# Retention attention into a SoLU layer: a negated copy of h with a row maximum, variance by squares on ScalarE, new engine orders

## The chip, the core and the metric

The kernel runs on one core of a Trainium2 chip. The metric is the device time of one execution in microseconds, the median of the runs shown. A core has a matrix engine (PE, with its weight load PEld), VectorE (DVE), ScalarE (ACT), GpSimd (POOL) and a sync engine (SP) that here only issues transfers. Each engine executes its own queue in order; instructions of different engines wait for one another by semaphores. [...]

## What is computed

Inputs `q`, `k`, `v` are 8 batches x 8 heads x 576 positions x 64, all float32. The reference, cut to what matters:

```python
scores = scale * np.matmul(q, k.transpose(0, 1, 3, 2))
ret = scores * Dmat            # causal, gamma_h ** (i - j)
x = (ret @ v), heads side by side            # 4608 x 512
h = x @ w_in                                 # 4608 x 1024
e = np.exp(h - h_max)                        # h_max: row maximum
solu = h * (e / (np.sum(e) + 1e-09))
ln = (solu - mu) / np.sqrt(var + 1e-06) * g_ln
out = ln @ w_out                             # 4608 x 512
```

The layer norm cancels any common factor of a row, so the kernel never divides by the sum of the exponentials: it carries `h * e` and scales the `1e-6` by the square of that sum.

## The kernel before, in words

The 4608 rows are cut into 18 windows: for each batch two windows of 256 positions, and for each four batches one window that collects their last 64 positions. A window has two **streams** (the two halves of the heads, 36 in all, number i) and two **token tiles** (128 rows each, 36 in all, number t).

The steps of a stream are named by letters in the code. `ldq`, `ldk`, `ldv` load 256 KB each (SP). `sq`, `sk` scale q and k by powers of gamma to f16, `cv` casts v; they run on POOL (for the first two streams `sq` is on DVE and `cv` on ACT). `T` transposes q and k (PE), `qe` copies them out (ACT), `S` makes scores (PE), `mask` multiplies them by the causal mask (DVE, line 382), `K` makes the state of a window (PE), `sa`, `sd` add it up (DVE), `sm`, `sc` scale and cast it (POOL), `I` and `V` make the output (PE), `xe` copies it out as `xT` (ACT).

The steps of a token tile:

- `M1` (PE, line 434): eight 128x512 products fill the PSUM tile `h`, of which there is one buffer.
- `ex` (ACT, line 447): `e = exp(h)` read from PSUM, with the row sum `se`.
- `so` (DVE, line 454): `solu = h * e` in f16, one input in PSUM and one in SBUF. It ends the use of `h`: the next tile's `M1` waits for it.
- `bn` (DVE, lines 460 and 464): two `bn_stats` and one `bn_aggr` give the mean and the variance. After the second tile of a window, two small instructions of 128x2 (lines 468 and 471) put variance and `1e-6 * se * se` together.
- `rs` (POOL, line 477): the power -1/2.
- `L` (PE, line 483) transposes `solu`, `le` (ACT) copies it out, `M2` (PE, line 507) multiplies by the output weights.
- `od` (DVE, line 515), for the first `NE` = 14 tiles only: takes the mean times the column sums of the weights (`nws`) off the product. From tile 14 on the weights themselves are centred (`w2c16`), and `od` falls away. `oe` (ACT, line 523) scales by `rs`, `out` (SP) stores.

The output weights are made ready beside the first tiles: `wg` multiplies the rows by the gain (four on DVE, four on ACT), `WM` sums the columns on PE, `nw0`, `nw1` copy the sums out (ACT), `wf` scales the float32 weights again (ACT, eight times) and `wp` adds the sums (POOL, line 578, eight times).

What stands in which order on an engine is decided when the program is built. Every step is an `op(name, engine, kind, deps, key, emit, bufs)`; an engine's steps are sorted by key and go into its queue in that order. The key is a formula in periods, or, for the steps listed in `FIRST`, their place in a list written out by hand. `order_ops` only merges the queues. Before, the lists cover roughly tiles 0 to 14, and the rest goes by formula. A buffer count (`CAP`) and the steps that release a buffer make further waits.

Of the kernel before, what the change touches and what calls it, by code (L numbers as in the profile page):

```python
# [9 lines left out]
FP = mybir.dt.float32  # L10
F16 = mybir.dt.float16
P = 128
# [4 lines left out]
    qe=0.6, xe=0.59, ex=1.22, le=0.6, oe=0.69, wi=0.6, wg=0.66, cva=0.6,  # L17
    mask=1.22, st_a=0.29, so=1.22, bn=1.68, od=0.7, wib=0.55, wgd=0.5, WM=1.73, nw=0.62, wf=0.66, wp=1.04, sqd=0.7, gc=0.2,
    sq=1.03, sk=1.03, st_b=0.4, cast=0.84, rs=0.6, cv=0.61,
# [6 lines left out]
NE = 14  # L26

FIRST = dict(
    ACT=(
        "cv0 qe0 cv1 qe1 xe0 wi1a wi2a wi0a xe1 wi3a ex0 qe2 wg0 le0 wg2 qe3 wg4 wg6 ex1 xe2 "  # L30
        "nw1 nw0 xe3 qe4 wf1 ex2 qe5 wf3 le1 xe4 qe6 wf2 ex3 le2 xe5 oe0 qe7 wf0 ex4 le3 xe6 "
        "qe8 ex5 le4 xe7 qe9 oe1 ex6 le5 oe2 qe10 xe8 ex7 le6 xe9 qe11 oe3 ex8 le7 oe4 wf6 "
        "qe12 xe10 wf4 ex9 le8 xe11 oe5 wf7 qe13 ex10 le9 xe12 wf5 qe14 oe6 ex11 le10 xe13 "
        "oe7 qe15 oe8 ex12 le11 xe14 qe16 oe9 ex13 le12 xe15 qe17 oe10 ex14 le13"
    ),
    DVE=(
        "gc sq0 sa0 sd0 sq1 mask0 wi1b sa1 sd1 mask1 wi2b wi0b wi3b sa2 sd2 so0 mask2 wg1 sa3 "
        "sd3 wg3 wg5 wg7 mask3 so1 bn0 sa4 sd4 bn1 mask4 so2 od0 sa5 sd5 mask5 bn2 sa6 sd6 "
        "so3 mask6 od1 bn3 sa7 sd7 so4 mask7 od2 bn4 sa8 sd8 so5 mask8 bn5 sa9 sd9 so6 od3 "
        "mask9 bn6 so7 od4 sa10 sd10 mask10 bn7 so8 od5 sa11 sd11 mask11 bn8 sa12 so9 sd12 "  # L40
        "od6 mask12 bn9 sa13 sd13 so10 od7 mask13 bn10 so11 sa14 sd14 od8 bn11 mask14 so12 "
        "sa15 sd15 od9 mask15 bn12 so13 od10 mask16 bn13 so14"
    ),
    PE=(
        "G K0 T0 S0 T1 I0 V0 K1 S1 I1 V1 M1_0 T2 K2 S2 L0 I2 V2 K3 T3 M1_1 S3 WM I3 V3 K4 T4 "
        "M1_2 S4 T5 M2_0 L1 I4 V4 K5 S5 T6 M1_3 I5 V5 K6 S6 L2 M2_1 T7 M1_4 I6 V6 K7 S7 L3 "
        "M2_2 T8 M1_5 I7 V7 K8 S8 L4 M2_3 T9 M1_6 I8 V8 K9 L5 S9 T10 M1_7 L6 I9 M2_4 V9 K10 "
        "S10 T11 M1_8 L7 I10 M2_5 V10 K11 S11 T12 M1_9 L8 I11 V11 K12 S12 M2_6 T13 M1_10 I12 "
        "V12 K13 S13 L9 M2_7 T14 M1_11 I13 L10 M2_8 V13 K14 S14 T15 M1_12 L11 M2_9 I14 V14 "
        "K15 S15 T16 M1_13 L12 I15 S16 V15 M2_10 T17 M1_14 L13 I16 S17 V16 M2_11"  # L50
    ),
    POOL=(
        "sk0 sk1 sm0 sc0 sm1 sc1 sq2 sk2 cv2 sk3 sm2 sc2 cv3 sq3 sm3 sc3 sk4 sq4 cv4 sq5 sk5 "
        "sm4 sc4 sq6 rs0 cv5 sk6 sq7 sm5 sc5 cv6 cv7 sk7 sm6 sk9 sc6 sk8 sq8 wp0 rs1 sm7 sc7 "
        "cv8 sq9 cv10 cv9 wp3 sm8 sk10 sc8 cv12 wp2 sq10 sq11 sq12 sm9 sc9 sk11 cv11 sk12 wp1 "
        "sm10 sc10 sk13 rs2 sq13 sq14 cv14 sm11 sc11 sk14 rs3 wp6 sm12 sc12 cv13 sq16 cv15 "
        "cv16 sm13 sc13 wp4 sk15 sq15 sk16 wp5 rs4 sm14 sc14 sq17 wp7 sk17 rs5 cv17 sm15 sc15 "
        "sq18 sk18 cv18 sq19 sk19 cv19"
    ),
    SP=(  # L60
        "ldk0 ldv0 ldq0 ldk1 ldq1 lm ldv1 lwi1 lwi2 lwi0 lwi3 ldq2 ldk2 ldv2 ldk3 lwo0 ldv3 "
        "ldq3 lwo2 lwo4 lwo6 ldk4 ldq4 ldv4 ldq5 ldk5 ldq6 ldv5 ldk6 ldv7 ldq7 ldq9 ldk7 ldk8 "
        "ldv6 ldq10 ldv8 ldk9 ldq11 ldq8 ldv10 ldk10 ldv11 ldq14 ldk11 ldk14 ldv9 ldv12 ldq12 "
        "ldk12 ldk13 ldq16 out0 out1 ldk17 ldv16 ldq15 ldq13 ldv13 out2 ldv14 ldq17 ldk16 "
        "out4 ldv15 ldk15 out3 out5 out7 out6 ldv17 ldv18 ldq19 ldk18 ldv19 ldq18 ldk19 ldq20 "
        "out8 ldk20 ldv20 out9 ldq21 ldk21 ldv21"
# [107 lines left out]
def kernel(  # L174
# [21 lines left out]
               xT=5, h=1, e=2, oc=2, solu=3, sml=8, lnT=4, o=1, osb=3)  # L196
# [28 lines left out]
    nws = const.tile([P, 2, DM], FP)  # L225
# [213 lines left out]

    def exp_(t):  # L440
        d = tk[t]
        w, c = divmod(t, 2)
        d["e"] = pools["e"].tile([P, DFF], FP, tag="e", name="e_sb")
        if c == 0:
            ws[w]["se"] = pools["sml"].tile([P, 2], FP, tag="se", name="se")
            ws[w]["mv"] = pools["sml"].tile([P, 2, 2], FP, tag="mv", name="mv")
        nc.scalar.activation(  # L447
            out=d["e"], in_=d["h"], func=ACT.Exp, accum_out=ws[w]["se"][:, c : c + 1]
        )

    def solu(t):
        d = tk[t]
        d["solu"] = pools["solu"].tile([P, DFF], F16, tag="solu", name="solu")
        nc.vector.tensor_tensor(out=d["solu"], in0=d["h"], in1=d["e"], op=ALU.mult)  # L454

    def stats(t):
        w, c = divmod(t, 2)
        bs = pools["sml"].tile([P, 2, 6], FP, tag="bs", name="bs")
        for half in range(2):
            nc.vector.bn_stats(  # L460
                out=bs[:, half], in_=tk[t]["solu"][:, half * 512 : half * 512 + 512]
            )
        d = ws[w]
        nc.vector.bn_aggr(out=d["mv"][:, c], in_=bs)
        if c:
            x = pools["sml"].tile([P, 2], FP, tag="w", name="w")
            d["x2"] = pools["sml"].tile([P, 2], FP, tag="w2", name="w2")
            nc.vector.scalar_tensor_tensor(  # L468
                out=x, in0=d["se"], scalar=1e-6, in1=d["se"], op0=ALU.mult, op1=ALU.mult
            )  # L470
            nc.vector.tensor_tensor(out=d["x2"], in0=x, in1=d["mv"][:, :, 1], op=ALU.add)  # L471
# [39 lines left out]
    def o_mean(t):  # L511

        d = tk[t]
        d["oc"] = pools["oc"].tile([P, DM], FP, tag="oc", name="oc")
        nc.vector.scalar_tensor_tensor(  # L515
            out=d["oc"], in0=nws[:, 0], scalar=ws[t // 2]["mv"][:, t % 2, 0:1], in1=d["o"],
            op0=ALU.mult, op1=ALU.add,
        )
# [58 lines left out]
    def w2_center(x):  # L577
        nc.gpsimd.tensor_tensor(out=w2c16[:, x], in0=w2_f[:, x], in1=nws[:, 1], op=ALU.add)
# [46 lines left out]
    for t in range(NT):  # L625
        w, c = divmod(t, 2)
        m = t + 2
        op(f"M1_{t}", "PE", "M1", [f"xe{2 * w}", f"xe{2 * w + 1}"] + [f"wi{x}{y}" for x in range(4) for y in "ab"],
           (m, 3.18), lambda t=t: mm1(t), [("h", [f"so{t}"])])
        op(f"ex{t}", "ACT", "ex", [f"M1_{t}"], (m, 5.1), lambda t=t: exp_(t), [("e", [f"so{t}"])])  # L630
        op(f"so{t}", "DVE", "so", [f"ex{t}"], (m + 1, 1.03), lambda t=t: solu(t), [("solu", [f"L{t}", f"bn{t}"])])
        op(f"bn{t}", "DVE", "bn", [f"so{t}", f"bn{t - 1}" if c else ""], (m + 1, 4.5), lambda t=t: stats(t))
        if c:
            op(f"rs{w}", "POOL", "rs", [f"bn{t - 1}", f"bn{t}"], (m + 2, 0.77), lambda w=w: rstd(w), [("sml", [f"oe{t}"])])
        op(f"L{t}", "PE", "L", [f"so{t}"], (m + 1, 4.9), lambda t=t: ln_tp(t), [("tp", [f"le{t}"])])
        op(f"le{t}", "ACT", "le", [f"L{t}"], (m + 2, 0.97), lambda t=t: ln_ev(t), [("lnT", [f"M2_{t}"])])
        o_end = f"od{t}" if t < NE else f"oe{t}"
        op(f"M2_{t}", "PE", "M2", [f"le{t}"] + [f"{'wg' if t < NE else 'wp'}{x}" for x in range(8)], (m + 4, 1.0),
           lambda t=t: mm2(t), [("s" if late(t) else "o", [o_end])])
        if t < NE:  # L640
            op(o_end, "DVE", "od", [f"M2_{t}", "nw0"], (m + 4, 2.9), lambda t=t: o_mean(t), [("oc", [f"oe{t}"])])
        op(f"oe{t}", "ACT", "oe", [o_end if t < NE else f"M2_{t}", f"rs{w}"], (m + 4, 3.6 if t < NE else 2.9),
           lambda t=t: o_ev(t), [("osb", [f"out{t}"])])
        op(f"out{t}", "SP", "out", [f"oe{t}"], (m + 4, 4.4 if t < NE else 3.6), lambda t=t: store(t))
# [8 lines left out]
    op("gc", "DVE", "gc", ["G"], (0, 1.0), lambda: nc.vector.tensor_copy(out=gln, in_=cur["g_ps"][:, 0:8]))  # L653
    for c in range(0, 8, 2):
        op(f"lwo{c}", "SP", "ldw", [], (-2 + c / 8, 0.6), lambda c=c: nc.sync.dma_start(out=w2_f[:, c : c + 2], in_=w2_v[:, c : c + 2]))
        for x in (c, c + 1):
            op(f"wf{x}", "ACT", "wf", ["gc", "nw1"], (8 + x * 0.75, 1.9), lambda x=x: nc.scalar.activation(
                out=w2_f[:, x], in_=w2_f[:, x], func=ACT.Copy, scale=gln[:, x : x + 1]))
            op(f"wp{x}", "POOL", "wp", [f"wf{x}"], (9 + x * 0.75, 1.9), lambda x=x: w2_center(x))
# [14 lines left out]
    with tc.manual_schedule():  # L674
# [4 lines left out]
        nc.vector.memset(minus1, -1.0)  # L679
# [3 lines left out]
        nc.vector.memset(warm, 0.0)  # L683
# [43 lines left out]
```

## Time and profile before

| | |
|---|---|
| runs | 227.62, 225.35, 226.4 us; median 226.4 |
| span of the profiled execution, first to last instruction | 225.6 us |
| mean granted PE clock | 0.988 |
| DMA | 42.64 MB, 189 GB/s over the span |
| `M1` of tile 0 / 3 / 15 / 31 / 35 starts at | 15.28 / 37.04 / 106.60 / 191.65 / 210.65 us |
| `ex` (line 447), 128x1024 from PSUM | 1022 ns, and 194 ns for reading out its row sum |
| `mask` (line 382), 128x1024 | 1215 ns |
| `od` (line 515), 128x512 | 740 ns |
| `wp` on POOL (line 578), 128x512 | 1268 ns |
| `sq`, `sk` on POOL (line 274) / `cv` (line 282) | 1040 / 608 ns |
| `sm` (line 407) / each half of `sc` (line 416) / `rs` (line 477) on POOL | 418 / 400 / 691 ns |

Beyond its span the page has no time for the profiled execution itself; the span lies 0.8 us under the median of the runs. The busy shares are averages over a start, a stretch in which tiles come irregularly, a regular stretch and an end, so the start times of `M1` are used to cut the span into stages. An instruction's duration counts from when its engine took it up, so it includes time in which it was held; back to back, DVE and ACT instructions start about 0.09 us before the end of the one ahead.

### The profile page before, as it was taken

How to read it: one execution, taken by the hardware profiler on the slowest of the kernel's cores; microseconds unless marked ns; L12 is line 12 of the kernel's file. 1: busy time of each engine (PE TensorE's matmuls, PEld its weight loads, DVE VectorE, ACT ScalarE, POOL GpSimd, SP SyncE). 2: the span in 40 equal slices, each digit the busy share in tenths (PEclk: the TensorE clock that was granted, in tenths of full speed). 3: DMA queues.
4: the chain of work that ended last, by engine and by line, in shares of the span. 5: the costliest groups of instructions: out<-in, count | busy, mean ns of one | idle time of the engine just before them, and what ended most of it. 6: DMA issues, size and time to landing. Idle time of an engine off the chain costs nothing.

```text
span 225.6 us, 7375 instructions
## 1 busy us (share of the span) xinstructions
PE 208.6 (92%) x2983; PEld 122.0 (54%) x2983; DVE 180.0 (80%) x320; ACT 133.2 (59%) x238; POOL 151.6 (67%) x231
## 2 busy tenths in 40 slices
PE   7876989999699999699999999999999999999991
PEld 2423555656355655465665666666566666555440
DVE  6655798999969898999999877778888888876540
ACT  2454776656457876466666566666665556655641
POOL 3439599999959989929669869695968777311010
PEclk9999999999799999999999999999999999999998
DMA  6999999995594600799987777777764552222334
GB/s 178 351 346 346 326 289 289 293 293 135 132 264 109 191 11 3 179 300 310 294 225 202 236 195 205 202 193 193 209 190 107 145 141 53 49 47 60 84 71 117
DMA packets 65635, 42.64 MB, mean 189 GB/s; under 512 B 4024, under 2 KB 59456, under 8 KB 65600
## 3 DMA queue, kind: packets, MB, share of 16 engines
q1 hardware_dynamic: 65200, 41.96, 67.7%
q8 instruction: 23, 0.38, 0.8%
q10 hardware_dynamic: 400, 0.21, 0.6%
q14 instruction: 12, 0.10, 0.2%
HBM read 32.71 MB, written 9.44 MB: 187 GB/s over the span
## 4 chain that ended last, share of the span: by engine, by line
PE 65%; DVE 17%; DMA 5%; POOL 4%; SPq 4%; issue 2%; ACT 1%; DVEq 0%; POOLq 0%; ACTq 0%
PE h_ps L434 22%; PE o_ps L507 21%; PE xy L314 7%; PE tln L483 5%; PE tqk L291 5%; DVE solu L454 4%; PE s_ps L349 4%; DVE bs L460 3%; DVE ret L382 3%; DMA vr<-in_v_dram 3%; SPq L259 3%; DMA masks<-masks 2%; DVE w L471 2%; DVE oc L515 2%; DVE w L468 1%
## 5 line engine op out<-in xcount | busy, mean ns | idle before, releaser
L434 PE MATMUL h_ps<-w_in,xT 128*128 128x512 f16 x288 | 69.7, 386 | 2.0 <-DVE solu L454 1.9
L454 DVE TENSOR_TENSOR solu<-h_ps,e_sb 128x1024 f16<-128x1024 f32 x36 | 43.9, 1219 | 19.2 <-ACT e_sb L447 19.0
L447 ACT ACTIVATE e_sb<-h_ps 128x1024 f32<-128x1024 f32 x36 | 36.8, 1022 | 31.6 <-PE h_ps L434 31.5
L460 DVE BATCH_NORM_STATS2 bs<-solu 128x6 f32<-128x512 f16 x72 | 46.0, 680 | 0.1
L382 DVE TENSOR_TENSOR ret<-s_ps,masks 128x1024 f16<-128x1024 f32 x36 | 43.8, 1215 | 0.2 <-issue 0.2
L434 PEld LDWEIGHTS <-xT 128*128 128x128 f16 x288 | 27.3, 99 | 30.0 <-issue 4.4
L274 POOL TENSOR_TENSOR k<-kr,small 128x512 f16<-128x512 f32 x36 | 37.5, 1041 | 6.9 <-DMA kr<-in_k_dram 5.1
L507 PEld LDWEIGHTS <-lnT 128*128 128x128 f16 x288 | 25.9, 98 | 27.2
L274 POOL TENSOR_TENSOR q<-qr,small 128x512 f16<-128x512 f32 x34 | 35.2, 1039 | 7.0 <-DMA qr<-in_q_dram 6.9
L507 PE MATMUL o_ps<-w2c,lnT 128*128 128x512 f16 x160 | 38.0, 380 | 0.0
L477 POOL TENSOR_TENSOR rs<-w,small 128x2 f32<-128x2 f32 x18 | 12.4, 691 | 30.0 <-DVE w L471 29.9
L299 ACT COPY qkT<-tqk 128x512 f32<-128x512 f32 x36 | 20.9, 580 | 12.6 <-PE tqk L291 12.6
L416 POOL CAST sbd<-g 64x256 f16<-64x256 f32 x64 | 25.6, 400 | 3.3
L507 PE MATMUL o_ps<-w2g,lnT 128*128 128x512 f16 x112 | 26.5, 379 | 0.0
L422 ACT CAST xT<-xy 128x512 f16<-128x512 f32 x36 | 21.4, 593 | 8.1 <-PE xy L314 6.8
L523 ACT ACTIVATE o_sb<-o_ps,rs 128x512 f32<-128x512 f32 x20 | 13.7, 687 | 20.8 <-PE o_ps L507 12.4
L407 POOL TENSOR_TENSOR g<-tt,small 128x128 f32<-128x128 f32 x32 | 13.4, 418 | 16.4 <-DVE tt L403 16.4
L483 PEld LDWEIGHTS <-solu 128*128 128x128 f16 x288 | 18.6, 98 | 9.3 <-DVE solu L454 2.0
L483 PE MATMUL tln<-ident,solu 128*128 128x128 f16 x288 | 22.1, 220 | 1.0 <-DVE solu L454 1.0
L491 ACT COPY lnT<-tln 128x512 f32<-128x512 f32 x36 | 20.8, 579 | 3.5 <-PE tln L483 3.5
L282 POOL CAST v<-vr 128x512 f16<-128x512 f32 x34 | 20.5, 608 | 1.7 <-DMA vr<-in_v_dram 0.3
L314 PE MATMUL xy<-ret,v 64*64 64x128 f16 x576 | 14.6, 219 | 2.0 <-DVE ret L382 2.0
(51 smaller groups left out, 241.7 us busy)
## 6 DMA issues: line engine op xcount, KB each, us to landing
kr<-in_k_dram SPq DMA_DIRECT2D x32, 256.0 KB, 4.9
vr<-in_v_dram SPq DMA_DIRECT2D x32, 256.0 KB, 5.0
qr<-in_q_dram SPq DMA_DIRECT2D x32, 256.0 KB, 4.8
out_dram<-o_sb SPq DMA_DIRECT2D x64, 128.0 KB, 2.4
w_in_f<-in_moe_w_in_dram SPq DMA_DIRECT2D x4, 512.0 KB, 6.8
w_f<-in_moe_w_out_dram SPq DMA_DIRECT2D x4, 512.0 KB, 7.6
qr<-in_q_dram SPq DMA_DIRECT2D x16, 64.0 KB, 2.2
kr<-in_k_dram SPq DMA_DIRECT2D x16, 64.0 KB, 2.7
```

The costliest lines, as they stand in the source:

```text
L274: eng.tensor_tensor(out=t.rearrange("p j h d -> p h j d"), in0=st[i][nm + "r"], in1=g_of(i, base), op=ALU.mult,)
L299: nc.scalar.copy(out=d["qkT"].rearrange("p n h j q -> p (n h j q)").bitcast(FP), in_=d["tp"].rearrange("p n h j q -> p (n h j q)").bitcast ...
L314: nc.tensor.matmul(start=(c, e) not in begun, stop=False, skip_group_check=True, **kw)
L382: nc.vector.tensor_tensor(out=d["ret"].rearrange("p e h j q -> p (e h) (j q)"), in0=d["s"].rearrange("p e h j q -> p (e h) (j q)"), in1=ma ...
L416: nc.gpsimd.tensor_copy(out=s16[ee[e], :, :, ee[e]], in_=st[i]["g"][ee[e]])
L422: nc.scalar.copy(out=d["xT"].rearrange("p c h q -> p c (h q)"), in_=d["av"][:, :, 0:256])
L434: nc.tensor.matmul(out=h_ps[:, hh], lhsT=st[2 * w + dc // 2]["xT"][:, c, dc % 2], rhs=w_in16[:, dc, hh], start=(dc == 0), stop=(dc == 3),)
L447: nc.scalar.activation(out=d["e"], in_=d["h"], func=ACT.Exp, accum_out=ws[w]["se"][:, c : c + 1])
L454: nc.vector.tensor_tensor(out=d["solu"], in0=d["h"], in1=d["e"], op=ALU.mult)
L460: nc.vector.bn_stats(out=bs[:, half], in_=tk[t]["solu"][:, half * 512 : half * 512 + 512])
L483: nc.tensor.transpose(out=tp[:, c], in_=d["solu"][:, c * P : (c + 1) * P], identity=ident)
L507: nc.tensor.matmul(out=d["o"], lhsT=d["lnT"][:, c], rhs=(w2g16 if t < NE else w2c16)[:, c], start=(c == 0), stop=(c == 7))
```

## The change

- `em` is new on DVE: it writes `hn = -h` from PSUM to SBUF in float32 and, as accumulator output, the row minimum `nm` of `hn`. It, not `so`, now ends the use of `h` in PSUM. `hn` has three buffers.
- `ex` reads `hn` from SBUF, with scale -1 and the bias `nm`.
- `so` reads `hn` and `e`, both from SBUF in float32, and gives the row sum `su` as accumulator output. Its product has the sign turned, which the gain with a turned sign (`gc`) makes up for.
- `va` is new on ACT: the square of `su - 1024 * solu`, with its row sum `sv`. It takes the place of the two `bn_stats` and the `bn_aggr` on DVE.
- `x` on DVE holds the two small instructions, once for each window, now with `sv`.
- `wf` falls away (eight ACT instructions), `nw0` and `nw1` become one `nw`, and `wp` moves from POOL to DVE as one instruction with two float32 inputs in SBUF.
- `FIRST` is new, and its lists now run through all 36 streams and tiles on every engine, in an irregular order: no step of the tiles after 14 is placed by formula any more.

```diff
 DUR = dict(
-    qe=0.6, xe=0.59, ex=1.22, le=0.6, ...
+    qe=0.6, xe=0.59, ex=1.25, em=1.3, va=1.25, x=0.3, le=0.6, ...
...
+WPOOL = ()
 FIRST = dict(
...
     DVE=(
-        "gc sq0 sa0 sd0 sq1 mask0 wi1b sa1 sd1 mask1 wi2b wi0b wi3b sa2 sd2 so0 mask2 wg1 sa3 "
-        "sd3 wg3 wg5 wg7 mask3 so1 bn0 sa4 sd4 bn1 mask4 so2 od0 sa5 sd5 mask5 bn2 sa6 sd6 "
...
+        "sq1 sq0 sa0 sd0 mask0 sa1 sd1 mask1 wi1b wi2b sa2 gc sd2 wi3b wi0b mask2 em0 sa3 sd3 so0 "
+        "em1 mask3 wg7 so1 sa4 sd4 mask4 em2 wg1 wg5 wg3 mask5 sa5 em3 sd5 so2 x0 wp3 wp0 sa6 od0 "
+        "sd6 mask6 em4 so3 od1 em5 sa7 sd7 mask7 so4 x1 od2 sa8 mask8 sd8 em6 od3 so5 sa9 mask9 "
+        "sd9 x2 wp6 em7 od4 mask10 sa10 sd10 so6 em8 od5 so7 em9 sa11 sd11 mask11 so8 od6 sa12 x3 "
...
+        "sa18 mask18 sd18 od13 wp1 so15 em17 mask19 wp5 sa19 od12 sd19 wp7 em16 x7 so17 sa20 sd20 "
...
     ),
...
-               xT=5, h=1, e=2, oc=2, solu=3, sml=8, lnT=4, o=1, osb=3)
+               xT=5, h=1, hn=3, e=2, oc=2, solu=3, sq=2, sml=8, lnT=4, o=1, osb=3)
...
+    def neg_max(t):
+        d = tk[t]
+        d["hn"] = pools["hn"].tile([P, DFF], FP, tag="hn", name="hn")
+        d["nm"] = pools["sml"].tile([P, 1], FP, tag="nm", name="nm")
+        nc.vector.tensor_scalar(
+            out=d["hn"], in0=d["h"], scalar1=-1.0, scalar2=None, op0=ALU.mult, op1=ALU.min,
+            accum_out=d["nm"],
+        )
     def exp_(t):
...
         nc.scalar.activation(
-            out=d["e"], in_=d["h"], func=ACT.Exp, accum_out=ws[w]["se"][:, c : c + 1]
+            out=d["e"], in_=d["hn"], func=ACT.Exp, scale=-1.0, bias=d["nm"],
+            accum_out=ws[w]["se"][:, c : c + 1],
         )
     def solu(t):
...
-        nc.vector.tensor_tensor(out=d["solu"], in0=d["h"], in1=d["e"], op=ALU.mult)
+        nc.vector.scalar_tensor_tensor(
+            out=d["solu"], in0=d["hn"], scalar=1.0, in1=d["e"], op0=ALU.mult, op1=ALU.mult,
+            accum_out=ws[w]["su"][:, c : c + 1],
+        )
+    def squares(t):
...
+        nc.scalar.activation(
+            out=x, in_=tk[t]["solu"], func=ACT.Square, scale=-float(DFF),
+            bias=ws[w]["su"][:, c : c + 1], accum_out=ws[w]["sv"][:, c : c + 1],
+        )
-    def stats(t):
...
-            nc.vector.bn_stats(
-                out=bs[:, half], in_=tk[t]["solu"][:, half * 512 : half * 512 + 512]
-            )
-        nc.vector.bn_aggr(out=d["mv"][:, c], in_=bs)
...
+    def stats(w):
...
+        nc.vector.scalar_tensor_tensor(
+            out=d["x2"], in0=d["sv"], scalar=float(DFF) ** -3, in1=x, op0=ALU.mult, op1=ALU.add
+        )
     def w2_center(x):
-        nc.gpsimd.tensor_tensor(out=w2c16[:, x], in0=w2_f[:, x], in1=nws[:, 1], op=ALU.add)
+        if x in WPOOL:
...
+        nc.vector.scalar_tensor_tensor(
+            out=w2c16[:, x], in0=w2_f[:, x], scalar=gln[:, x : x + 1], in1=nws, op0=ALU.mult, op1=ALU.add
+        )
...
-           (m, 3.18), lambda t=t: mm1(t), [("h", [f"so{t}"])])
-        op(f"ex{t}", "ACT", "ex", [f"M1_{t}"], (m, 5.1), lambda t=t: exp_(t), [("e", [f"so{t}"])])
...
+           (m, 3.18), lambda t=t: mm1(t), [("h", [f"em{t}"])])
+        op(f"em{t}", "DVE", "em", [f"M1_{t}"], (m, 5.1), lambda t=t: neg_max(t), [("hn", [f"so{t}"])])
+        op(f"ex{t}", "ACT", "ex", [f"em{t}"], (m + 1, 1.1), lambda t=t: exp_(t), [("e", [f"so{t}"])])
+        op(f"so{t}", "DVE", "so", [f"ex{t}"], (m + 1, 2.4), lambda t=t: solu(t), [("solu", [f"L{t}", f"va{t}"])])
+        op(f"va{t}", "ACT", "va", [f"so{t}"], (m + 1, 4.5), lambda t=t: squares(t))
...
+            op(f"x{w}", "DVE", "x", [f"va{t - 1}", f"va{t}"], (m + 2, 0.6), lambda w=w: stats(w))
```

## The prediction

> **What bounds the kernel now.** I read the page's busy rows first, then the busy time by stage (cut at the starts of `M1`), then the rows of the costliest groups, then the order of time where DVE and POOL meet.
>
> ```profile
> PE 208.6 (92%) x2983; PEld 122.0 (54%) x2983; DVE 180.0 (80%) x320; ACT 133.2 (59%) x238; POOL 151.6 (67%) x231
> DVE  6655798999969898999999877778888888876540
> POOL 3439599999959989929669869695968777311010
> ```
>
> The reader is to see that DVE and POOL are nearly full in much of the first half (mostly nines from slice 6 to 21) and have room in the second. Cut at `M1` of tiles 3, 15 and 31:
>
> ```profile
> core 0: us, PE busy (x) PEld busy (x) DVE busy (x) ACT busy (x) POOL busy (x), PEclk, DMA share, GB/s
> 37.04:106.60 69.56, 65.23 (x966) 38.56 (x964) 64.24 (x105) 43.62 (x78) 59.54 (x86) 0.98 0.70 188
> 106.60:191.65 85.05, 85.05 (x1332) 52.60 (x1332) 71.92 (x132) 52.09 (x97) 65.11 (x102) 1.00 0.69 187
> ```
>
> The early stretch is 12 tiles in 69.56 us, 5.80 a tile; DVE is busy 5.35 of that (92%), POOL 4.96. The regular stretch is 16 tiles in 85.05, 5.32 a tile; PE is busy all of it, DVE 4.50, POOL 4.07, ACT 3.26. So the early stretch hangs on DVE (the chain of waits goes over `solu`, `ret`, `oc`, `bs` there), the regular one on PE.
>
> The next lines, in order of time, decide my forecast.
>
> ```profile
> 55.62 1.27 POOL L578 TENSOR_TENSOR w2c<-w_f,nws 128x512 f16<-128x512 f32 x1
> ...
> 55.81 1.09 DVE L468 SCALAR_TENSOR_TENSOR w<-se 128x2 f32<-128x2 f32 x1
> ...
> 56.85 3.04 POOL L274 TENSOR_TENSOR q<-qr,small 128x512 f16<-128x512 f32 x3
> ...
> 56.94 0.97 DVE L471 TENSOR_TENSOR w<-w,mv 128x2 f32<-128x2 f32 x1
> ```
>
> ```profile
> 114.97 0.11 DVE L468 SCALAR_TENSOR_TENSOR w<-se 128x2 f32<-128x2 f32 x1
> ...
> 115.11 0.16 DVE L471 TENSOR_TENSOR w<-w,mv 128x2 f32<-128x2 f32 x1
> ```
>
> Lines 468 and 471 work on two elements a row. With POOL idle they take 0.11 and 0.16 us; beside POOL 1.09 and 0.97, and they end where POOL's instruction ends (55.62 + 1.27 = 56.89; 56.85 + 3.04/3 = 57.87). Both have two inputs in SBUF. `bn_aggr`, just as small but with one input, takes 208 to 211 ns in all 36 cases, and `solu` and `mask`, with one input in PSUM, keep to 1.22 whatever POOL does. It works the other way too:
>
> ```profile
> 8.25 0.76 DVE L274 TENSOR_TENSOR q<-qr,small 128x512 f16<-128x512 f32 x1 [0.48 <-DMA qr<-in_q_dram]
> ```
>
> ```profile
> 8.42 0.85 POOL L407 TENSOR_TENSOR g<-tt,small 128x128 f32<-128x128 f32 x1
> ```
>
> That DVE instruction has two SBUF inputs; POOL's `sm`, normally 0.40, waits until it is over. So such DVE instructions and POOL's exclude each other. Before, only the small pair (36 instructions) pays: 8.2 us in the early stretch (0.68 a tile), 2.1 in the regular one (0.13).
>
> **The change part by part.** `so` becomes an instruction of that kind, 36 times at full size; so do the eight `wp` on DVE. I call the time that POOL and these instructions need together the shared time.
>
> DVE, per tile. Off: `bn`, 1.44 (from the start of `bn_stats` to that of line 468, 113.53 to 114.97). On: `em`, 1.13, the spacing of `solu`, the nearest row (128x1024 from PSUM). Two accumulator outputs on DVE have no row; ACT's read takes 0.19, of which 0.10 shows when it is followed at once, so 0 to 0.19 each, taken 0.10. Waiting of `so`: if POOL is in an instruction all the time, a random arrival waits for the sum of squares over twice the sum of its instructions of a tile (1.04, 1.04, 0.61, and 8/9 of 0.40, 0.40, 0.40, and half of 0.69): 3.19 / 8.2 = 0.39. It can be 0 (POOL idle) and 1.04; I take 0.39. `wp`: the spacing of a 128x512 `od`, 0.65, plus 0.39, 1.04 each; five stand in the list between `em3` and `em15`, three later. Behind a held `so` there wait, on DVE, the next `mask` (V, then `xe`, need it), `em` (frees `h`), and `sa`, `sd` (POOL's `sm`, and then `I`).
>
> Early stretch: 5.35 - 1.44 + 1.13 + 0.20 + 0.39 + 5 x 1.04 / 12 (0.43) = 6.06 a tile. DVE fully packed gives 6.06 (+3.1 us over 12 tiles); with the 0.45 of idle that it has now 6.51 (+8.5). I take 6.3, **+6.0**. POOL there: 4.96 - 0.84 (eight `wp` of 1.27 less) + 1.13 + 0.27 = 5.5, below that.
>
> Regular stretch: DVE 4.50 - 1.44 + 1.13 + 0.20 + 0.39 = 4.78, plus three `wp` (0.20) and the small pair, which goes from 0.13 towards 0.68 (taken +0.27): 5.25, just under PE's 5.32. The shared time: POOL 4.07 + `so` 1.13 + the pair 0.13 + `wp` 0.12 = 5.45, just over it. Today POOL is idle 1.25 a tile, mostly waiting for DVE's `w` (29.9 us in the row of waits) and `tt` (16.4); that idleness is what `so` would have to fit into. Ends: all fits, 5.32, +0; half of the idleness stays, 6.05, +11.7. I take 5.55, **+3.7**.
>
> ACT: off, eight `wf` and one `nw`, early, where ACT is 63% busy: nothing. On, per tile: `va`, and a dearer `ex`. From rows: a bias from SBUF 0.10 (722 against 620 ns at 128x512), an input in SBUF rather than PSUM 0.03 (620 against 593). `ex` 1.15, `va` about 1.15 and 0.19 for its sum: 3.26 + 0.13 + 1.34 = 4.73, under 5.32; hidden by PE in the regular stretch, at a price of up to 0.5 a tile if ACT's order fails to keep that cover. `x` now waits for `va`, so DVE may stand at `x`; the list puts it behind `so` and `em` of later tiles, and I price it at nothing, bounded by one `va`, 1.3 per window.
>
> The early release of `h`: PE waited for `solu` before `M1` 1.9 us in four cases in all, so it can earn no more than that; `em` stands in the same DVE queue, behind `so` and `mask`. Two of those waits (0.29 each) are at the end: **-0.5**, between -0.6 and +1.3 (one more DVE step between the last `M1` and its `L`). The start (tiles 0 to 2) gains 1.44 and loses 1.13 + 0.2 a tile: nothing, within 1 us either way. Transfers are the same 42.64 MB; their buffers come free when POOL has scaled, so they follow POOL. No DMA is moved to another queue. `gc`, `minus1`, `nw`: nothing, one instruction each.
>
> Sum: 225.6 + 6.0 + 3.7 - 0.5 = 234.8 of span; the median of the runs lies 0.8 above the span, so **235.6 us**. The ends give 228 to 247.
>
> [...]
>
> **The rivals.** *Faster: DVE is relieved.* If `so` is mostly taken up while POOL is idle, as the small pair is in the regular stretch, there is no wait and the pair's 0.55 goes too: DVE in the early stretch needs 5.35 - 1.44 + 1.13 + 0.20 + 0.27 - 0.55 = 4.96, less than PE's 5.32, so PE sets the pace: 12 x 0.48 = 5.8 less, with the end 225.6 - 6.3 + 0.8 = 220. For it: POOL idles 1.25 a tile in the regular stretch. Against: POOL is busy 86% of the early stretch, and the shared time is over 5.32. It decides from a mean `so` under about 1.35 us.
>
> *No change:* half of that relief early is given back by POOL later: 226.
>
> *Much slower: `so` at a lower rate.* The slowest row for two float32 SBUF inputs is POOL's, 1.04 for 128x512, so 2.08 for `so`, 0.86 more on DVE and in the shared time. Early 7.16 a tile (+16.3), regular 6.41 (+17.4), other tiles about +3: 263.
>
> **How the numbers follow.** The forecast has 0.60, relief 0.18, no change 0.12, the slow `so` 0.10. One per cent (2.3 us) is about what a measurement can tell from no change here. Faster by more: 0.15 (relief, but for its upper edge). Within: 0.10 of no change, 0.03 of relief, 0.02 of the forecast's low end, 0.15. Slower: the rest, 0.70. The range 222 to 248 leaves out half of the relief case below (0.09) and the slow `so` above (0.10). The cases of slower hold most by far.
>
> **What would show it.** Right: `solu` has a spread of durations from 1.2 up past 2, mean about 1.6 to 1.7, ending with POOL's instructions; POOL's `q`, `k`, `v` rows stretch in mean and maximum; the regular tiles take over 5.4. Wrong: `solu` at 1.2 to 1.3 throughout with POOL unstretched (relief); all `solu` over 2 with POOL idle (the slow `so`); DVE and POOL with room and ACT at nine tenths, which none of my cases has.

## The result, and the profile after

The changed kernel takes 247.1 us (245.58 to 248.75) against 226.8: ratio 1.091, 95% interval 1.084 to 1.099. Its profiled execution took 246.69 us, of which the span is 244.9. Where the single runs of a kernel below fall into two groups (the upper one mostly at a lower granted clock), its time and ratio are those of the lower group.

| stage, cut at the starts of `M1` | before | after | change |
|---|---|---|---|
| up to tile 3 | 37.04 | 35.48 | -1.6 |
| tiles 3 to 15 | 69.56 (5.80 a tile) | 76.19 (6.35) | +6.6 |
| tiles 15 to 31 | 85.05 (5.32) | 97.74 (6.11) | +12.7 |
| from tile 31 | 33.91 | 35.50 | +1.6 |

Two thirds of the loss are in the regular stretch, which was PE's own before. From the page of after, the busy row and PE's row of slices:

```profile
PE 214.4 (88%) x2998; PEld 124.1 (51%) x2998; DVE 182.9 (75%) x328; ACT 172.2 (70%) x301; POOL 172.7 (71%) x223
...
PE   8968887998997788999799889899869999999992
```

No engine is full any more: PE has sevens and eights in the middle. The busy time by stage, cut at tiles 3, 15 and 31, says it in numbers (columns as in the prediction):

```profile
35.48:111.67 76.19, 66.90 (x978) 39.06 (x971) 66.54 (x115) 56.93 (x100) 62.59 (x79) 1.00 0.69 188
111.67:209.41 97.74, 87.99 (x1280) 51.91 (x1273) 73.56 (x131) 71.92 (x126) 80.07 (x100) 0.98 0.55 152
```

In the regular stretch PE stands still for 9.8 us, DVE for 24, ACT for 26, and POOL for 18, in spite of all its stretched instructions. So the reading is that a chain through several engines, one after the other, sets this stretch. The rows of waits of the whole execution name it (who waited, for whom: us in all, times, longest):

```profile
POOL g L441 <- DVE tt L437: 30.2, 18, 7.2
PEld L348 <- POOL sbd L450: 22.0, 20, 3.1
ACT xT L456 <- PE xy L348: 19.0, 16, 2.7
PE xy L348 <- POOL sbd L450: 15.8, 17, 2.6
```

In the regular stretch alone (111.67 to 209.41 us), most of PE's 9.8 us are in this row:

```profile
PE xy L348 <- POOL sbd L450: 7.1, 7, 2.6
```

POOL's `sm` (line 441) waits for DVE's `sd` (437), PE's `I` (348) for POOL's `sc` (450): that is the state of a stream on its way from `K` over `sa`, `sd`, `sm`, `sc` to the `I` of the same stream. `V` comes behind that `I`, and the program makes the next stream's `K` wait for that `V`, so the way closes into a loop, once for each stream. Before, PE waited so little for `sc` that the wait stood in none of the ten largest rows. In the chain that ended last, POOL's share went from 4% to 31% and PE's from 65% to 33%.

The lock that the prediction was built on is there, mostly on the other engine. Three rows of the costliest groups (before: `solu` about 1.22, `k` 1041 ns, `v` 608):

```profile
L501 DVE SCALAR_TENSOR_TENSOR solu<-hn,e_sb 128x1024 f16<-128x1024 f32 x36 | 47.7, 1326 | 5.3 <-ACT e_sb L491 5.3
...
L308 POOL TENSOR_TENSOR k<-kr,small 128x512 f16<-128x512 f32 x36 | 42.1, 1175 | 4.3 <-DMA kr<-in_k_dram 3.6
...
L316 POOL CAST v<-vr 128x512 f16<-128x512 f32 x34 | 27.1, 801 | 0.8 <-PE xy L348 0.2
```

In order of time, near 144 us (start, duration, instruction, idle before and what ended it):

```profile
143.72 1.23 DVE L501 SCALAR_TENSOR_TENSOR solu<-hn,e_sb 128x1024 f16<-128x1024 f32 x1 [0.45 <-ACT e_sb L491]
143.77 2.07 POOL L308 TENSOR_TENSOR q<-qr,small 128x512 f16<-128x512 f32 x1
...
145.79 0.60 POOL L316 CAST v<-vr 128x512 f16<-128x512 f32 x1
...
146.35 0.85 POOL L450 CAST sbd<-g 64x256 f16<-64x256 f32 x2
...
147.25 0.28 PE L348 MATMUL xy<-qkT,sbd 128*128 128x128 f16 x2 [1.15 <-POOL sbd L450]
```

`solu` starts 0.05 us before POOL's `q`, takes its usual 1.23, and `q` takes 2.07 instead of 1.04. Behind `q` in POOL's queue stands `v`, behind that `sc`, and for `sc` PE waits 1.15.

### The profile page after: what moved, and what is told of

Same layout as the page of the kernel before. It is cut to its first block, busy times and chain, and to the rows that moved or that the text cites. A ratio compares the mean times of both kernels' runs of the same rounds, so it can differ in the third digit from the quotient of the medians.

```text
span 244.9 us, 7426 instructions
## 1 busy us (share of the span) xinstructions
PE 214.4 (88%) x2998; PEld 124.1 (51%) x2998; DVE 182.9 (75%) x328; ACT 172.2 (70%) x301; POOL 172.7 (71%) x223
## 4 chain that ended last, share of the span: by engine, by line
PE 33%; POOL 31%; DVE 13%; DMA 9%; issue 7%; ACT 5%; SPq 1%; POOLq 0%; DVEq 0%; ACTq 0%
POOL sbd L450 9%; PE h_ps L468 8%; POOL k L308 7%; PE o_ps L560 7%; POOL q L308 6%; PE xy L348 6%; POOL g L441 4%; DMA qr<-in_q_dram 4%; POOL v L316 3%; PE tln L536 3%; DVE ret L416 3%; DMA out_dram<-o_sb 2%; PE tqk L325 2%; DVE hn L479 2%; PE wm L755 2%
## 5 line engine op out<-in xcount | busy, mean ns | idle before, releaser
L501 DVE SCALAR_TENSOR_TENSOR solu<-hn,e_sb 128x1024 f16<-128x1024 f32 x36 | 47.7, 1326 | 5.3 <-ACT e_sb L491 5.3
L479 DVE TENSOR_SCALAR_CACHE_REDUCE hn<-h_ps 128x1024 f32<-128x1024 f32 x36 | 43.8, 1218 | 9.9 <-PE h_ps L468 9.8
L491 ACT ACTIVATE e_sb<-hn,nm 128x1024 f32<-128x1024 f32 x36 | 41.4, 1151 | 8.0 <-DVE hn L479 6.2
L308 POOL TENSOR_TENSOR k<-kr,small 128x512 f16<-128x512 f32 x36 | 42.1, 1175 | 4.3 <-DMA kr<-in_k_dram 3.6
L510 ACT ACTIVATE sq<-solu,su 128x1024 f32<-128x1024 f16 x36 | 41.3, 1148 | 1.2 <-DVE solu L501 1.2
L308 POOL TENSOR_TENSOR q<-qr,small 128x512 f16<-128x512 f32 x34 | 39.4, 1165 | 3.7 <-DMA qr<-in_q_dram 3.0
L441 POOL TENSOR_TENSOR g<-tt,small 128x128 f32<-128x128 f32 x32 | 17.1, 534 | 30.7 <-DVE tt L437 30.2
L450 POOL CAST sbd<-g 64x256 f16<-64x256 f32 x64 | 34.8, 544 | 3.0
L530 POOL TENSOR_TENSOR rs<-w,small 128x2 f32<-128x2 f32 x18 | 15.2, 846 | 20.3 <-DVE w L519 12.7
L348 PE MATMUL xy<-qkT,sbd 128*128 128x128 f16 (+1 forms) x128 | 13.5, 214 | 16.4 <-POOL sbd L450 15.8
L316 POOL CAST v<-vr 128x512 f16<-128x512 f32 x34 | 27.1, 801 | 0.8 <-PE xy L348 0.2
```

Source lines behind the costliest of these rows:

```text
L308: eng.tensor_tensor(out=t.rearrange("p j h d -> p h j d"), in0=st[i][nm + "r"], in1=g_of(i, base), op=ALU.mult,)
L316: copy(out=t, in_=st[i]["vr"])
L348: nc.tensor.matmul(start=(c, e) not in begun, stop=False, skip_group_check=True, **kw)
L450: nc.gpsimd.tensor_copy(out=s16[ee[e], :, :, ee[e]], in_=st[i]["g"][ee[e]])
L479: nc.vector.tensor_scalar(out=d["hn"], in0=d["h"], scalar1=-1.0, scalar2=None, op0=ALU.mult, op1=ALU.min, accum_out=d["nm"],)
L491: nc.scalar.activation(out=d["e"], in_=d["hn"], func=ACT.Exp, scale=-1.0, bias=d["nm"], accum_out=ws[w]["se"][:, c : c + 1],)
```

## The experiments

Theories: **(lock)** POOL stretched by `so` makes the loss, whatever the order; **(loop)** the state's loop over three engines has become too long for a tile and sets the pace; **(order)** the new lists put the steps in a bad order, which costs even without the lock. The columns after the ratio are of one profile each: the start of `M1` of tile 3, us per tile in the two stretches, and the time from tile 31. The profile of regular_od_behind_so is of an execution of 233.2 us.

| label | us | ratio (95%) | tile 3 at | 3 to 15 | 15 to 31 | end |
|---|---|---|---|---|---|---|
| the change | 247.1 | 1.091 (1.084-1.099) | 35.5 | 6.35 | 6.11 | 35.5 |
| one_input | 234.2 | 1.033 (1.029-1.037) | 34.4 | 6.02 | 5.68 | 35.4 |
| before_two_inputs | 237.7 | 1.047 (1.043-1.052) | 39.1 | 6.37 | 5.39 | 34.0 |
| loop_cut | 240.1 | 1.057 (1.051-1.062) | 35.1 | 6.42 | 5.66 | 35.6 |
| formula_order | 249.0 | 1.100 (1.093-1.107) | 36.0 | 6.54 | 6.04 | 36.4 |
| so_after_mask | 243.0 | 1.071 (1.062-1.081) | 36.1 | 6.67 | 5.63 | 35.2 |
| so_after_mask_one_input | 237.6 | 1.049 (1.041-1.057) | 34.9 | 6.35 | 5.59 | 35.4 |
| so_after_mask_f16 | 242.7 | 1.072 (1.064-1.080) | 35.5 | 6.67 | 5.63 | 35.4 |
| so_after_mask_early | 249.2 | 1.099 (1.089-1.109) | 36.0 | 7.12 | 5.61 | 34.7 |
| regular | 238.9 | 1.052 (1.044-1.059) | 35.6 | 6.70 | 5.36 | 34.8 |
| regular_one_input | 234.5 | 1.032 (1.023-1.041) | 34.5 | 6.50 | 5.36 | 34.8 |
| regular_so_before_mask | 247.3 | 1.089 (1.082-1.096) | 35.9 | 6.97 | 5.71 | 35.1 |
| regular_from_6 | 238.8 | 1.052 (1.044-1.059) | 35.4 | 6.76 | 5.36 | 34.8 |
| regular_wp_pool | 236.2 | 1.043 (1.036-1.050) | 36.1 | 6.46 | 5.39 | 34.8 |
| regular_wp_pool_ne10 | 238.8 | 1.055 (1.048-1.061) | 36.2 | 6.81 | 5.32 | 34.8 |
| regular_od_behind_so | 229.5 | 1.013 (1.003-1.023) | 35.4 | 6.35 | 5.32 | 34.8 |
| regular_od_behind_so_wp_pool | 235.8 | 1.039 (1.033-1.046) | 35.4 | 6.52 | 5.35 | 34.7 |
| od_behind_so_one_input | 230.2 | 1.015 (1.009-1.021) | 34.5 | 6.18 | 5.32 | 34.7 |
| od_behind_so_from_5 | 228.6 | 1.011 (1.006-1.016) | 40.8 | 5.52 | 5.32 | 34.7 |

The state's loop, read from the order of time of each stream that lies whole in the regular stretch (14 or 15 streams): medians from the start of `K` to that of `sd`, to that of `sm`, through `sm` and `sc` to the end of `sc` (the loop), and from there to the next `K` (the rest).

| kernel | `K` to `sd` | to `sm` | `sm` and `sc` | loop | rest | streams with a loop over 4.57 |
|---|---|---|---|---|---|---|
| before | 1.68 | 0.37 | 1.29 | 3.41 | 1.96 | 0 of 15 |
| the change | 1.45 | 0.37 | 2.27 | 5.44 | 0.82 | 8 of 14 |
| one_input | 1.44 | 0.37 | 1.96 | 4.51 | 0.84 | 7 of 14 |
| before_two_inputs | 1.76 | 1.51 | 1.29 | 4.17 | 1.17 | 4 of 15 |
| formula_order | 3.55 | 0.37 | 1.29 | 5.22 | 0.74 | 15 of 15 |
| regular_so_before_mask | 0.75 | 1.68 | 2.28 | 4.71 | 0.95 | 8 of 15 |
| regular | 0.75 | 0.66 | 1.30 | 3.05 | 2.27 | 0 of 15 |
| od_behind_so_from_5 | 0.75 | 0.65 | 2.19 | 3.59 | 1.67 | 0 of 15 |

(Medians of parts don't add up. In the change the streams scatter: loops of 2.4 to 8.8 us, mean 5.25.) `I`, `S` and `V` stand between `sc` and the next `K` and take about 0.75. So a loop longer than 5.32 - 0.75 = 4.57 is estimated to hold PE up, and the rest then shrinks towards these 0.75. The rows agree: where no stream is over 4.57 a regular tile takes 5.32 to 5.36, with four of fifteen 5.39, and with half of them or more 5.68 to 6.11.

**one_input.** `so` leaves out the factor `hn`: one SBUF input, the same size, the same accumulator.

```diff
-        nc.vector.scalar_tensor_tensor(
-            out=d["solu"], in0=d["hn"], scalar=1.0, in1=d["e"], op0=ALU.mult, op1=ALU.mult,
+        nc.vector.tensor_scalar(
+            out=d["solu"], in0=d["e"], scalar1=1.0, scalar2=None, op0=ALU.mult, op1=ALU.add,
```

> The changed kernel, with solu made from e alone (one SBUF input, same size, same accumulator output); the factor hn is left out. Nothing else is moved, so the engine orders are the same. Theory A (the lock between solu and POOL, which lengthens POOL's instructions, makes the regular tiles slow): POOL's total busy time falls from 172.7 to about 142 us, the regular tiles (M1 of tile 15 to tile 31) from 6.11 to 5.3-5.5 us, the kernel to 228-234 us. Theory B (the new orders are slow by themselves, the lock only sits in idle time): POOL's instructions shrink all the same, but the tiles stay at 5.9 us or more and the kernel over 241 us.

```profile
L501 DVE TENSOR_SCALAR_CACHE_REDUCE solu<-e_sb x36: 1203/1212/1221, 25.7 to 220.6; 128x1024 f16<-128x1024 f32 x36
```

```profile
L308 POOL TENSOR_TENSOR k<-kr,small x36: 1036/1042/1045, 4.3 to 198.9; 128x512 f16<-128x512 f32 x36
```

The two lines give one tile's and one line's instructions (min/median/max ns): `solu` has no spread left, and POOL's `k` ends at 1045, where it reached 2108 in the change. That takes 12.9 us off (247.1 to 234.2), and leaves 7.3 that are not `so`'s lock (the eight `wp` and `x` still have two inputs in SBUF): regular tiles at 5.68, although POOL is busy only 63.1 of the 90.9 us of that stretch.

**before_two_inputs.** The kernel before, with `solu = e * e`.

```diff
-        nc.vector.tensor_tensor(out=d["solu"], in0=d["h"], in1=d["e"], op=ALU.mult)
+        nc.vector.tensor_tensor(out=d["solu"], in0=d["e"], in1=d["e"], op=ALU.mult)
```

> The kernel before, with solu = e * e (two SBUF inputs); the factor h is left out, so h is also released by exp rather than by solu. Its orders, bn_stats and weights stay. Theory A: POOL's instructions stretch by up to 1 us where they meet solu, about 25-35 us in sum, and the kernel goes from 227 to 232-242 us. Theory B: POOL has 1.25 us of idle time a tile here and a regular order; the kernel stays within 1% of 227 us.

The lock costs 10.7 us here, but nearly all of it in the start and the early tiles. The regular tiles keep to 5.39, although `so` waits longer than in the change (mean 1414 ns) and POOL is busier (177.4 us of 235.7). So the lock does not by itself make regular tiles of 6.11.

**loop_cut.** `I` multiplies by zeros instead of the state, so PE does not wait for `sc`; all else runs on.

```diff
-                    mm(d["begun"], c, 0, out=oo, lhsT=s16[:, hp], rhs=d["qkT"][:, 0, hp, :, qq])
+                    mm(d["begun"], c, 0, out=oo, lhsT=zeros[:, :P], rhs=d["qkT"][:, 0, hp, :, qq])
```

> The changed kernel, with the products of q and the carried state (line 348, I) reading a constant zero tile instead of the state that POOL casts; the contribution of the earlier window is left out. POOL does the same work under the same lock, but PE no longer waits for POOL's sc. If the slowness comes by the loop K, sa, sd, sm, sc, I, V, K (5.28 us from K to the end of sc in the changed kernel, 3.49 before), the tiles fall to about the shared time of POOL and solu, 5.4-5.6 us, and the kernel to 230-236 us. If POOL's throughput under the lock is the bound, the kernel stays at 243-248 us.

The loop is worth 7.0 us, all in the regular stretch (5.66 instead of 6.11) and none in the early one. That is less than expected of it: with the loop open, PE still waits 3.1 us there for POOL's `q`, `k` and `v` and 1.4 for ACT's `xT`. The granted clock in that stretch was 0.98 in the change's profile and 1.00 here, so a part of the difference may be the clock; PE's idle time alone fell from 9.8 to 5.3 us.

**formula_order.** The lists end at period 16; from there the formula keys that the change itself gives order the steps.

```diff
+LIM = dict(ld=21, sq=18, K=16, sa=16, sm=16, I=15, M=14, em=14, ex=13, so=13, L=13, od=10, oe=10)
...
+FIRST = {e: " ".join(n for n in l.split() if early(n)) for e, l in FIRST.items()}
```

> The changed kernel, with the lists of the engine orders cut off at period 16: steps after that are placed by the formula keys, as in the kernel before. Work and lock are the same. Theory A: the lock meets a regular order instead of an irregular one, the tiles after 15 stay at 5.8 us or more, the kernel at 240-250 us. Theory B: the tiles after 15 come back to 5.3-5.6 us and the kernel to 233-238 us.

Not faster, so the irregular lists are not the whole cause (without `so`'s lock this order was not tried). But this order repeats every tile, and its cycle can be read:

```profile
165.85 1.22 DVE L494 TENSOR_SCALAR_CACHE_REDUCE hn<-h_ps 128x1024 f32<-128x1024 f32 x1
...
167.16 0.29 PE L363 MATMUL xy<-v,k 64*64 64x64 f16 x16
167.17 1.15 ACT L506 ACTIVATE e_sb<-hn,nm 128x1024 f32<-128x1024 f32 x1 [0.88 <-DVE hn L494]
...
168.44 1.74 DVE L516 SCALAR_TENSOR_TENSOR solu<-hn,e_sb 128x1024 f16<-128x1024 f32 x1 [1.37 <-ACT e_sb L506]
...
170.11 0.28 DVE L445 COPY g<-xy 128x128 f32<-128x128 f32 x1
...
172.22 0.29 PE L363 MATMUL xy<-qkT,sbd 128*128 128x128 f16 x2 [0.31 <-POOL sbd L465]
```

`K` starts at 167.16, but `sa` (`g<-xy`) waits until 170.11, because `so` stands ahead of it in DVE's queue, DVE stands idle 1.37 us for `ex`, and `so` then takes 1.74, held by POOL's `k` (168.06 to 169.10). Only then come `sa`, `sd`, `sm`, `sc`, and PE's next `I` at 172.22. Three engines in a row, with `so` inside the loop.

**so_after_mask, and with one input, earlier, and in f16.** As formula_order, but `so` goes behind `mask`, and what hangs on it follows.

```diff
-        op(f"so{t}", "DVE", "so", [f"ex{t}"], (m + 1, 2.4), ...
-        op(f"va{t}", "ACT", "va", [f"so{t}"], (m + 1, 4.5), ...
+        op(f"so{t}", "DVE", "so", [f"ex{t}"], (m + 1, 4.0), ...
+        op(f"va{t}", "ACT", "va", [f"so{t}"], (m + 2, 0.2), ...
```

> The changed kernel with the lists cut off at period 16, and in the formula that follows so is moved from before the state steps (key 2.4) to behind mask (key 4.0), va to the start of the next period, x behind mask, rs behind sc. Work and lock as in the changed kernel. DVE then runs sa, sd, mask, so, em, and e is ready a whole cycle before so; sm and sc run beside mask, where nothing holds them. If the regular tiles are slow because so's hold and its place in the order meet the state's loop, they come to 5.3-5.5 us (6.11 in the changed kernel, 6.0 with the formula as it was) and the kernel to 237-241 us. If the lock alone costs POOL too much throughput, they stay at 5.8 us or more, the kernel over 244 us.

From tile 18 on every tile takes 5.32, with the lock in force. Only the passage (tiles 14 to 17, 6.4 to 7.2 each) and the early tiles, whose order the list still gives, are left slow; with them the kernel misses the expected 237-241.

> The same order, with solu made from e alone (the factor hn is left out), so without so's lock. If the lock is harmless in this order, the regular tiles are the same within 0.1 us as with it, and only the tiles before 16 gain (about 6 us, as one_input gained there): 231-234 us. If the lock still costs in a regular order, the tiles are shorter by 0.3 us or more than with it.

Tiles 18 to 31 take 5.32 here too, so in this order the lock costs nothing there; most of the 5.5 us between the two kernels lie ahead of tile 15 (1.2 in the start, 3.8 in the early tiles).

> The same formula from period 8 on already; the eight wp then go by formula too. If the irregular lists are what costs in the tiles before 16 as well, these go from 6.35 to 5.9 us or less and the kernel comes under so_after_mask by 3 us or more. If DVE's sum (6.06 a tile with od and wp) bounds them, the kernel is within 2 us of so_after_mask, or slower.

The same with the lists cut at period 8: regular from early on, but 7.12 a tile in the early stretch. The order that serves tiles without `od` does not serve those with it.

> As so_after_mask, with hn and e stored in f16 instead of float32: so's two inputs have half the bytes. If the length of so follows the bytes, it falls from 1.21 to about 0.7 us when it is not held, its hold on POOL shrinks the same way, and the kernel gains 2-6 us over so_after_mask, mostly before tile 16. If this form goes at one element a cycle whatever the type, so stays at 1.21 and the kernel within 1 us.

`hn` and `e` in f16: 242.7 us, against 243.0 in float32. No gain.

**regular, and around it.** Cut at period 8, `od` just behind `mask` (key 3.4), `wp` one a tile behind it (3.45), `so` at 4.0. regular_one_input has the edit of one_input, regular_so_before_mask `so` at 3.0, regular_from_6 the cut at 6.

```diff
-            op(o_end, "DVE", "od", [f"M2_{t}", "nw"], (m + 4, 2.9), ...
+            op(o_end, "DVE", "od", [f"M2_{t}", "nw"], (m + 4, 3.4), ...
...
-               (7 + x * 0.5, 1.9), lambda x=x: w2_center(x))
+               (9 + x, 3.45), lambda x=x: w2_center(x))
```

> As so_after_mask_early (formula from period 8, so behind mask), with od moved behind mask (key 3.4; at 2.9 it stood in front of mask and DVE waited for M2 there), and the eight wp one a period from period 9 on, behind od. All the work and the lock of the changed kernel are in it. If orders that make DVE stand still were the cost, the tiles from 8 to 18 go from 6.9 to 5.4-5.9 us and the kernel to 226-236 us, 10 us or more under the changed kernel. If DVE's or POOL's sum is the bound early, they stay at 6.2 us or more, the kernel over 239 us.

> As regular, with solu made from e alone (hn left out): the price of so's lock in an order that fits. If the lock has a price only where the order gives it one, this is within 2 us of regular (the tiles before 8, still by list, keep some). If the lock costs as such, 6 us or more below.

> As regular, with so between the state steps and mask (key 3.0) instead of behind mask: so starts when sm is about to start, and holds it. If what hurts is so meeting sm and sc, the way from K to the end of sc grows by about 1 us and the regular tiles from 5.32 to 5.6 us or more, the kernel by 6 us or more. If that growth fits into the 2.3 us that the loop has to spare at 5.32, the tiles stay within 0.1 us and only DVE standing still decides.

> As regular, with the lists cut off at period 6 already. If the irregular lists cost as much in the tiles 4 to 7 as in the later ones, another 2-4 us are gained; if the lists suit the start (weights and first loads), it is within 1.5 us or slower. Best case under the kernel before, 226 us.

regular saves 8.2 us of the change, less than expected (tiles 8 to 18 take 6.22), and the lock costs 4.4 in it (238.9 against 234.5), none of it after tile 15 (5.36 in both). Moving `so` alone to a place ahead of `mask` costs 8.5 (247.3), as much as the whole gain of the order; by the profiles 5.6 of it lie in the regular stretch. The loop goes from 3.05 to 4.71, since `sm` and `sc` are then POOL's instructions beside `so`. Cutting earlier changes nothing. What is left of the early stretch can be seen in the order of time of regular:

```profile
70.26 0.75 DVE L584 SCALAR_TENSOR_TENSOR oc<-nws,su,o_ps 128x512 f32<-128x512 f32 x1
...
70.92 0.88 DVE L650 SCALAR_TENSOR_TENSOR w2c<-w_f,gln,nws 128x512 f16<-128x512 f32 x1
...
71.73 1.62 DVE L517 SCALAR_TENSOR_TENSOR solu<-hn,e_sb 128x1024 f16<-128x1024 f32 x1
...
73.42 0.62 PE L552 MATMUL tln<-ident,solu 128*128 128x128 f16 x8 [1.02 <-DVE solu L517]
```

`od` and `wp` (1.5 us) stand ahead of `so`, and PE waits 1.02 for `so` before `L`.

**regular_wp_pool and regular_wp_pool_ne10.** `wp` on POOL again, from period 9, with `wf` on ACT; then `NE` = 10 as well, with `wp` from period 6.

```diff
-WPOOL = ()
+WPOOL = tuple(range(8))
```

> As regular, with the weights centred on POOL again (wf on ACT, wp on POOL, one a period from period 9 on, behind sc), as in the kernel before. DVE loses eight instructions of about 0.85 us, POOL gets eight of 1.27 us. If DVE's sum holds the tiles 8 to 18 at 6.35 us, they fall by 0.6-0.8 us and the kernel by 5-7 us, to 232-234 us. If POOL (under the lock) or the chain so, L, M2 on PE holds them, nothing is gained or the kernel is slower than regular, 238-243 us.

> The same with the weights centred from period 6 on and od for the first 10 tiles only (NE = 10): four more 128x512 instructions less on DVE. If DVE's sum holds the early tiles, the four tiles without od come at 5.4 us or less and the kernel gains another 2-4 us. If not, it is within 1.5 us of regular_wp_pool.

The move back gains 2.6 us; POOL is then busy 49.0 of the 51 us from 64 to 115. With `NE` = 10 the gain is gone; the eight `wp` then stand in earlier tiles, and whether that is the reason was not tried.

**od behind so.** As regular, with `od` (key 4.2) and `wp` (4.3) behind `so`, and `oe` at 6.4. Then with `wp` on POOL; with the edit of one_input; and with the lists cut at period 5 and `WM` and `nw` placed by formula too.

```diff
-            op(o_end, "DVE", "od", [f"M2_{t}", "nw"], (m + 4, 3.4), ...
+            op(o_end, "DVE", "od", [f"M2_{t}", "nw"], (m + 4, 4.2), ...
```

> As regular, with od and wp behind so instead of in front of it (keys 4.2 and 4.3), and oe later on ACT to match. Same work and the same sum on DVE, same lock. In regular, PE stood 8.3 us at L for so in tiles 5 to 18, and so stood behind od, which waits for M2. If that chain (M2, od, wp, so, L, then I, V, K and the next M2) holds the early tiles, they fall from 6.35 to 5.9 us or less and the kernel by 4 us or more, to 230-235 us. If DVE's sum holds them, they stay at 6.2 us or more and the kernel within 2 us of 238.9.

> The same with the weights centred on POOL (wf on ACT). If the chain holds the early tiles and DVE's sum comes next, this is another 3-5 us faster than regular_od_behind_so, 226-231 us. If POOL is then the bound under the lock (it was busy 49.0 of 51.0 us there in regular_wp_pool), it is no faster than regular_wp_pool, 236 us.

> As regular_od_behind_so, with solu made from e alone (hn left out). It gives the price of so's lock in the best order so far, beside 12.9 us in the changed kernel's order and 4.4 us in the order of regular. If the price comes by the order, it is 1-4 us (226-229 us), most of it in the tiles before 8. If the lock has a price of its own, 5 us or more (225 us or less).

> As regular_od_behind_so, with the lists cut off at period 5 (WM and nw by formula too). Tiles 3 to 6 took 24.6 us there and 16.8 in the kernel before; in the list, em stands between sa and sd of a stream, and so is late. If the list's order is the cause there too, 3-6 us are gained: 224-227 us, level with the kernel before or under it. If the weights' preparation and the loads hold these tiles, it stays at 229-231 us.

All of the change's work, with its lock, runs in 229.5 us in this order. Tiles 8 to 18 fall from 6.22 to 5.70, and PE's wait for `so` before `L` in the early stretch from 10.1 us to 3.0; tiles 3 to 6, still by list, gain nothing (22.9 and 24.6 us). `wp` on POOL costs 6.3 here, where it gained before; POOL is then busy 49.2 of the same 51 us. Without the lock the time is 230.2, no shorter, but at a granted clock of 0.98 to 0.99 against 1.00 with it, so what the lock costs ahead of tile 15 in this order stays open. From tile 15 to 31 it costs nothing: both take 5.32. The last kernel is the best one found, and still 1% above the kernel before. Its busy time from 110 to 195 us, and its order of time:

```profile
110.00:195.00 85.00, 85.00 (x1340) 52.46 (x1328) 70.41 (x131) 74.48 (x130) 79.37 (x104) 1.00 0.66 181
```

```profile
153.44 1.22 DVE L432 TENSOR_TENSOR ret<-s_ps,masks 128x1024 f16<-128x1024 f32 x1
...
153.88 0.40 POOL L457 TENSOR_TENSOR g<-tt,small 128x128 f32<-128x128 f32 x1
...
154.34 1.73 POOL L466 CAST sbd<-g 64x256 f16<-64x256 f32 x2
...
154.57 1.24 DVE L517 SCALAR_TENSOR_TENSOR solu<-hn,e_sb 128x1024 f16<-128x1024 f32 x1
```

PE is busy all 85 us with POOL busy 79.4 of them: the stretched instructions are still there, and cost nothing. `sm` runs beside `mask`, which has one input in PSUM and does not hold it (`sm` keeps its 0.40); `so` comes after, and what it stretches (the second half of `sc`) has slack. `ex` has had the time of `sa`, `sd` and `mask` to finish, so DVE doesn't stand at `so` either.

## Why the prediction was right and where it was wrong

**The direction and the lock held, the size did not.** Forecast were 235.6 us, with a range of 222 to 248; measured were 247.1. `so` and POOL's instructions exclude each other, and one_input puts 12.9 us on that in the change's order. That 247.1 lies just inside the range is luck: the upper end of the regular stretch, 6.05 a tile, was for half of POOL's idleness staying. Nearly all of it stayed (1.10 us a tile of 1.25) beside longer instructions, and what held the tiles was something else.

**The step that failed is the regular stretch: "I take 5.55, +3.7".** It measured 6.11 and +12.7. The step asked whether the sums fit (DVE 5.25, shared time 5.45, against PE's 5.32) and found them nearly fitting. They do fit: od_behind_so_from_5 runs the same work at 5.32. What the step lacked is the length of a path. The median loop went from 3.41 to 5.44, against the 4.57 that PE can bear; its part for `sm` and `sc` went from 1.29 to 2.27, and in single streams `sd` starts up to 6.0 us after `K`. The new lists, which the step gave no price, have a share in it: without `so`'s lock they still make a loop of 4.51 and regular tiles of 5.68, which is 5.9 of the 12.7 us; the lock in these lists makes the other 6.8. The runs show both parts: loop_cut takes 7.0 us off by opening the loop alone, and regular_so_before_mask puts 8.5 on by the place of `so` alone. The loop is not all of the 12.7: opened, it leaves regular tiles at 5.66, with waits for POOL's `q`, `k`, `v` and for `xT`, and these were not taken apart. The step had half of the thought: it listed `sa`, `sd` and `sm` as queued behind a held `so`, and gave them no price.

**The size of the lock on DVE** was taken as 0.39 us for each `so`; it was 0.11 (1326 against 1219 unheld), and the mean of 1.6 to 1.7 was wrong with it. POOL carries the waiting: per tile 0.13 for `k`, 0.12 `q`, 0.18 `v`, 0.26 `sc`, 0.10 `sm`, 0.08 `rs`, in all 0.87. The estimate let only `so` arrive at random and find POOL busy; it did not ask who arrives while `so` runs.

**The relief rival** was to decide "from a mean `so` under about 1.35 us". The mean was 1.33, and the relief did not come. The test looked at the engine that was held less.

**The early stretch** was +6.6 against +6.0, for another reason than the one given. DVE was to be the bound at 6.06 a tile; it was busy 66.54 / 12 = 5.55, and idle more than before. PE waited there for `sc` (6.7 of its 9.3 us of idle time). loop_cut doesn't shorten this stretch (6.42), so the loop alone is not what holds it; with `od` behind `so` and shorter lists it runs at 5.52, though there tile 3 starts 5.3 us later and a part of the work has only moved ahead of it (tile 15 starts at 107.0 against 111.7). A right size, then, by luck, from a reason that the runs don't support.

**Start and end**, priced at 0 and -0.5, were -1.6 and +1.6 and cancel; neither was traced to a cause. Beside a span of 244.9 there lie 1.8 us, not the 0.8 that came from comparing the span of before with a median of other runs: 1.0 of the error.

**Small terms** held: `em` 1218 ns and 81 for its row minimum (taken 1.13 in spacing and 0.10), `ex` 1151 (1.15), `va` 1148 and 192 (1.15 and 0.19), `wp` 860 on DVE; ACT, 4.5 a tile in the regular stretch, did not become the bound. The sum left `so` at the rate of the old `solu` (1219 ns, one input in PSUM); no run of before shows the new form, with two SBUF inputs and an accumulator. In the change its shortest takes 1208 ns for 1024 elements a row, as much as one_input's, with one SBUF input and an accumulator (1203). The slow rival started from a misread row: the slowest for two float32 SBUF inputs was `wp` on POOL, 1268 ns, not 1040; and its 7.16 a tile is not the sum of the terms given (6.06 + 0.86 = 6.92).

**Still open:** in the best order tile 3 starts at 40.8 us, 3.7 later than before, while the early tiles are 0.28 faster each; the two nearly cancel at tile 15 (107.0 against 106.6). Whether the list or the weight preparation sets that start was not tried.

## What to carry to other kernels

Price an instruction that locks another engine by what stands around it, not by sums: look up which of the other engine's instructions will run beside it, and who waits for those. Measure every loop that runs through several engines once per tile, and compare it with the tile less what must follow. Here a loop below that bound cost nothing, and every order with half of its loops over it had slow tiles. Look at the single passes too, since a median hides the long ones. In an in-order queue put an instruction that waits for a slow partner behind those that a loop needs.

## What the runs showed of the hardware

- Either side may be held: POOL's 1.04 us instruction takes up to 2.11 when `so` is first (`k` at 152.45 us of the change, `so` at 152.44), and `so` up to 2.06 when POOL is first (`so` at 30.47, `k` at 30.23). In one_input, with one SBUF input at the same size, no POOL `k` goes over 1.05.
- A DVE accumulator read takes 75 to 84 ns in the change, against about 190 on ACT.
- f16 in place of float32 for both inputs of `so` gained nothing: 242.7 us (so_after_mask_f16) against 243.0 (so_after_mask).
